# Attention rounds of a fused kernel: second score pieces behind the transposes, a fourth output buffer, GpSimd work tied to later VectorE steps

## The chip, the cores and the metric

The kernel runs on one core of a Trainium2 chip. The metric is device time in microseconds (us). The kernel before took 706.64 us (median of three runs, 706.31 to 711.38).

## The reference: what is computed

An attention with a learned position bias feeds a feed-forward layer with a rational activation:

```python
scores = scale * q @ k.T                     # batch 4, heads 8, sequence 576, head width 64
bias = relu(psi(i, j) * w1 + b1) @ w2        # one value per pair of positions and head
attn = exp(scores + bias - rowmax)
attn = attn / (attn.sum(-1) + 1e-9)
x = (attn @ v)                               # as 2304 tokens x 512
h = x @ w_in                                 # 512 -> 2048
P = a0 + a1 h + a2 h^2 + a3 h^3
Q = 1 + |b0| |h| + |b1| h^2
out = (P / (Q + 1e-6)) @ w_out               # 2048 -> 512
```

## The kernel before, in words

The program has three parts: bias tables (up to about 50 us), attention, and the feed-forward layer. The change touches the attention part alone. All order is written out by hand (`manual_schedule`): each engine runs its instructions in the order in which the program text issues them, and waits inside that order.

**Units and steps.** A unit is a pair of heads of one batch element; there are 16 (`NU`). Two units share nine steps (`UPG = 9`): the even unit has five blocks of query rows (`c` from 0 to 4), the odd one four, because the fifth step carries the last 64 rows of both units (step 4 of nine, "the shared step"). So there are 72 steps (`NS`), and `rnd(r)` handles two, `i = 2r` and `i + 1`; rounds 1 to 35 are the attention's main loop.

**One round.** TensorE does, in this order: scores of step i and the long pieces of the scores of step i+1 (`e_qk`, L346; 576 columns are cut into 448 and 128 because they lie across two PSUM banks); then 32 transposes of the probabilities of steps i-2 and i-1 (`e_tp`, L433; the two halves of the rows, r = 0 and 1, are woven so that they can run side by side), with small ones for the tail columns and, where a unit has ended, for its row sums; the short second pieces (128 columns) of the scores of step i+1 stand among them; then the products with v for steps i-3 and i-2 (`e_pv`, L492). VectorE adds the bias and takes the row maximum (`e_ttr`, L365, one per head and step: four in a round), copies tail columns and row sums out of PSUM (`put_tails`, L460 and L469), turns sums into reciprocals (L389, L390) and copies products out of PSUM into the output buffer `xs` (L501). ScalarE does the exponentials (L379) and copies the transposes out of PSUM (L448).

**Output buffers.** Each unit has a tile `xs` of 128x576 in a pool of three buffers. It is filled a block at a time over its steps; when its row sums have come back from DRAM as `rb`, GpSimd multiplies it by them (`e_norm`, L414, in two halves of 288 columns, each in a round of its own), and SyncE (SP) sends it to DRAM as `xd` (L416). The first copy into the `xs` of a later unit waits until the transfer of the unit three before has left the buffer. A unit's product for an even step is put at the start of the next round (`puts`), that of an odd step near the end of its round.

**Weight passes.** Between these, from round 4 to round 33, weights of the feed-forward layer are split into a high and a low part, one pair of jobs (a, b) in three rounds (`job_plan`, phases 0, 1, 2). The passes of a job are: `mag` (VectorE, L156), `rebias` (ScalarE, L165), `sign` (VectorE, L168), `mid` (GpSimd, L177), `join` (VectorE, L181) and `low` (GpSimd, L188). VectorE's `sign` and `join` each read two tiles in SBUF. `behind(x, op)` makes a GpSimd instruction x wait for the VectorE instruction op, so that it doesn't run beside what stands ahead of it.

**Order of VectorE before, in a round:** put of the even step's product; early weight passes; the two `e_ttr` of step i; the two of step i+1; tails and sums; reciprocals; put of the odd step's product; later weight passes.

Of the kernel before, what the change touches and what calls it, by code (L numbers as in the profile page):

```python
# [9 lines left out]
F32 = mybir.dt.float32  # L10
# [7 lines left out]
P = 128  # L18
# [19 lines left out]
def tile_attn_moe(  # L38
# [91 lines left out]
    def w_conv(f, part):  # L130
# [36 lines left out]
        def sign():  # L167
            V.scalar_tensor_tensor(  # L168
                out=st["wh"], in0=rows(st["u"]), scalar=0x80000000, in1=st["wh"],
                op0=ALU.bitwise_and, op1=ALU.bitwise_or,  # L170
            )
# [61 lines left out]
    with tc.manual_schedule():  # L233
# [3 lines left out]
        with ExitStack() as actx:  # L237
# [121 lines left out]
            def e_ttr(i, j):  # L359
# [4 lines left out]
                o0 = strip(i, j)  # L364
                on(V.tensor_tensor_reduce(  # L365
                    out=t, in0=WF[:, o0:o0 + S], in1=bias[p][:, 5 * j + c, :],
                    scale=-0.125, scalar=3.0e38,
                    op0=ALU.add, op1=ALU.min, accum_out=m,
                ), o0 // 512, o0 // 512 + 1)
                s2[i, j] = (t, m)  # L370

            def e_exp(i, j):
# [34 lines left out]
            def e_norm(u):  # L407
# [10 lines left out]

                if eng is V:
                    return [lambda: part(0, S)]  # L420
                return [lambda: part(0, SH), lambda: part(SH, S)]

# [58 lines left out]
            def e_pv(i, b):  # L481
# [13 lines left out]
                for x in zs:  # L495
                    if x not in xs:
                        xs[x] = npool.tile([P, S], F32, tag="xs", name=f"xs{x}", bufs=3)

# [39 lines left out]
            def done_to(k):  # L538
                g, c = divmod(k, UPG)
                u = 2 * g - 2  # L540
                if g > 0:
                    if c == 1 and u != NX or k == NS:
                        norms.extend(e_norm(u))
                    if c == 6 and g * 2 < NU:
                        norms.extend(e_norm(u + 1))
                    if c == 2 and u + 1 < NU - 1:
                        load_rb(u + 1)
# [20 lines left out]
            def job_plan(r):  # L568
                q, ph = divmod(r - 4, 3)
                c = 2 * q  # L570
                if r < 4 or c >= len(jobs):
                    return [], [], [], [], []
                a, b = jobs[c], jobs[c + 1]
# [12 lines left out]
                if ph == 0:  # L586
                    return a[1], a[2], [a[4]], [a[3][0], hi(a)], []
                if ph == 1:
                    return [a[3][1]] + b[1], b[2], [a[3][2], b[4]], [b[3][0], hi(b)], [out(c)]
                return [b[3][1]], [], [b[3][2]], [], [out(c + 1)]  # L590

            ZZ = (4, 1)

            def rnd(r):
                i = 2 * r
                early, act, pool, later_, outs = job_plan(r)
# [4 lines left out]
                for x in early:  # L601
                    op = x() or op
                for x in act:
                    x()
# [34 lines left out]
                if put:  # L639
                    put()  # L640
                for x in later_ + list(hi[1:]) + outs:
                    x()
# [431 lines left out]
```

## Time and profile before

| what | us |
|---|---|
| median of three runs | 706.64 |
| profiled execution | 708.67 |
| its span, first to last instruction | 706.9 |
| rounds 2 to 35 of the attention | 246.99 |
| from the end of round 35 to the end | 404.00 |

The profiled execution was 2.03 us (0.3%) slower than the median, and 1.8 us of it lie outside the span. Round numbers are those of `rnd(r)`; a round is counted from the first of its scores on TensorE to the first of the next round's. In the views, PE is TensorE, DVE VectorE, ACT ScalarE, POOL GpSimd; a release in square brackets tells how long the engine had been idle and what ended it.

### The profile page before, as it was taken

To read this page: it belongs to the slowest core of one execution; us is meant where nothing else is said; L and a number is where in the kernel's file an instruction comes from. 1 tells how busy PE (TensorE), PEld (TensorE's weight loads), DVE (VectorE), ACT (ScalarE), POOL (GpSimd) and SP (SyncE) were. 2 spreads that over 40 slices of the span, in tenths; PEclk is the share of its full clock that TensorE was granted. 3 is DMA by queue.
4 is the path that set the end of the run, shared out by engine and by line. 5 is a ranking of instruction groups with operands and counts; after the bars stand their busy time and mean duration, and the time that the engine had idled before them with its cause. 6 is when DMAs were issued, how large, how long until landed. Compare 5 with 4: busy or idle time off the path is not lost.

```text
span 706.9 us, 16149 instructions
## 1 busy us (share of the span) xinstructions
PE 672.3 (95%) x6274; PEld 551.5 (78%) x6274; DVE 557.0 (79%) x1030; ACT 474.0 (67%) x758; POOL 155.4 (22%) x122
## 2 busy tenths in 40 slices
PE   9999969898988878999999999999999999999997
PEld 6657758667776657798888888899998888888896
DVE  7986867677756757749999898988877968779766
ACT  7979867777767758866676756656666564555551
POOL 0000223132312323202222212131221221221221
PEclk9999998999989989999999999999999999999999
DMA  6987766667667747643365361766850121303031
GB/s 232 307 315 241 247 187 227 196 223 209 203 184 253 230 165 221 201 132 121 116 183 190 118 207 48 254 209 203 301 181 29 59 105 60 104 1 119 1 105 45
DMA packets 74844, 118.97 MB, mean 168 GB/s; under 512 B 11904, under 2 KB 33808, under 8 KB 74768
## 3 DMA queue, kind: packets, MB, share of 16 engines
q1 hardware_dynamic: 74624, 117.79, 50.7%
q8 instruction: 49, 0.80, 0.5%
q14 instruction: 27, 0.22, 0.1%
q10 hardware_dynamic: 144, 0.16, 0.1%
HBM read 79.17 MB, written 35.61 MB: 162 GB/s over the span
## 4 chain that ended last, share of the span: by engine, by line
PE 61%; DMA 2%; DVE 1%; issue 1%; SPq 1%; POOL 0%; DVEq 0%
PE ps L316 28%; PE ps L903 28%; PE ps L492 2%; DMA xd<-xs 2%; PE ps L346 1%; PE ps L433 1%; DVE s L365 1%; DVE xs L501 0%; DVE wh L168 0%; POOL wm L177 0%; SPq L140 0%; SPq L128 0%; DVE wk L156 0%; DVE wm L181 0%; DVE pre L924 0%
## 5 line engine op out<-in xcount | busy, mean ns | idle before, releaser
L873 POOL TENSOR_TENSOR gl<-m,r 128x1024 fp32r<-128x1024 f32 (+1 forms) x39 | 85.6, 2195 | 300.0 <-DVE m L866 267.8
L365 DVE CUSTOM_DVE_ANT_0 s<-ps,bias 128x576 f32<-128x576 f32 x144 | 106.1, 756 | 23.6 <-PE ps L433 10.9
L346 PE MATMUL ps<-k,q 64*128 64x448 f32 (+3 forms) x640 | 108.3, 431 | 6.9 <-DVE m L365 6.7
L824 ACT ACTIVATE w<-ps,babs 128x1024 f32<-128x1024 f32 (+1 forms) x40 | 41.3, 1031 | 107.6 <-PE ps L316 104.0
L379 ACT ACTIVATE p<-s,m 128x576 f32<-128x576 f32 x144 | 110.1, 778 | 2.6 <-DVE m L365 2.6
L448 ACT COPY pt<-ps 128x512 f32<-128x512 f32 (+1 forms) x109 | 73.0, 730 | 42.0 <-PE ps L433 41.6
L433 PEld LDWEIGHTS ps<-ident,p 64*128 64x128 f32 x1296 | 62.4, 145 | 41.6 <-issue 33.4
L433 PE MATMUL ps<-ident,p 64*128 64x64 f32 x1296 | 68.7, 233 | 21.6 <-DVE xs L501 21.6
L492 PE MATMUL ps<-pt,v 128*64 128x128 f32 (+1 forms) x1280 | 85.4, 281 | 0.3 <-ACT pt L448 0.3
L903 PE MATMUL ps<-wol,gh 128*128 128x512 f32 x216 | 84.2, 390 | 0.0
L903 PE MATMUL ps<-woh,gh 128*128 128x512 f32 x216 | 84.2, 390 | 0.0
L346 PEld LDWEIGHTS ps<-k,q 64*128 64x128 f32 (+1 forms) x640 | 54.7, 178 | 31.9 <-issue 18.2
L836 DVE SCALAR_TENSOR_TENSOR u<-w,babs,ps 128x1024 f32<-128x1024 f32 (+1 forms) x40 | 46.9, 1172 | 38.1 <-ACT t L825 38.0
L492 PEld LDWEIGHTS ps<-pt,v 128*64 128x64 f32 x1280 | 71.8, 146 | 3.2 <-ACT pt L448 0.4
L316 PE MATMUL ps<-xb,wih 128*128 128x512 f32 (+1 forms) x240 | 68.8, 367 | 0.0
L501 DVE COPY xs<-ps 128x128 f32<-128x128 f32 (+1 forms) x80 | 21.0, 266 | 60.5 <-DMA xd<-xs 36.1
L831 ACT ACTIVATE u<-u 128x1024 f32<-128x1024 f32 (+1 forms) x40 | 39.1, 977 | 40.2 <-DVE u L836 40.1
L852 DVE SCALAR_TENSOR_TENSOR gh<-t,cst,r 128x1024 fp32r<-128x1024 f32 (+1 forms) x40 | 46.9, 1174 | 9.3 <-ACT r L833 6.9
L903 PE MATMUL ps<-woh,gl 128*128 128x512 f32 x216 | 53.8, 389 | 0.0
L859 DVE SCALAR_TENSOR_TENSOR m<-u,qc,gh 128x1024 f32<-128x1024 f32 (+1 forms) x40 | 47.1, 1178 | 4.0
L316 PEld LDWEIGHTS ps<-xb,wih 128*128 128x128 f32 x240 | 44.5, 188 | 6.1
L866 DVE SCALAR_TENSOR_TENSOR m<-t,cst,m 128x1024 f32<-128x1024 f32 (+1 forms) x40 | 47.1, 1178 | 1.4
(81 smaller groups left out, 1351.7 us busy)
## 6 DMA issues: line engine op xcount, KB each, us to landing
tab<-e SPq DMA_DIRECT2D x36, 295.5 KB, 3.2
wx<-in_w_in_dram SPq DMA_DIRECT2D x16, 512.0 KB, 5.0
wx<-in_w_out_dram SPq DMA_DIRECT2D x16, 512.0 KB, 4.5
v<-in_vp_dram SPq DMA_DIRECT2D x16, 320.0 KB, 3.7
ws<-wh SPq DMA_DIRECT2D x20, 256.0 KB, 2.0
ws<-wl SPq DMA_DIRECT2D x20, 256.0 KB, 3.1
q<-in_qt_dram SPq DMA_DIRECT2D x16, 288.0 KB, 3.6
k<-in_kt_dram SPq DMA_DIRECT2D x16, 288.0 KB, 4.6
```

What stands on the lines that cost most here:

```text
L316: on(T.matmul(hps[s][:, j, :w_], w[:, k, sl], x[:, k, :w_], start=(k == 0 and z == 0), stop=(k == KD - 1 and z == 2),), b + j)
L346: on(T.matmul(WF[o, o0 + a:o0 + z], q[r, x], k[r, a:z], start=True, stop=True), (o0 + a) // 512)
L365: on(V.tensor_tensor_reduce(out=t, in0=WF[:, o0:o0 + S], in1=bias[p][:, 5 * j + c, :], scale=-0.125, scalar=3.0e38, op0=ALU.add, op1=ALU.m ...
L379: A.activation(out=prob[i][:, z * S:z * S + S], in_=t, func=AF.Exp, bias=m, scale=-1.0, accum_out=sums[u % 4][:, k:k + 1],)
L433: on(T.transpose(W[:, b, o:o + 64], src[x, :], ident[x, x]), b)
L448: on(A.copy(out=t.rearrange("p x (r s) -> p r x s", r=2)[:, a:z], in_=W[:, to[a]:to[a] + z - a].rearrange("p r (x s) -> p r x s", s=64),), ...
L492: on(T.matmul(ps[y, o], vt[n][:, kc, y], w_, start=(kc == 0), stop=(kc == 4)), b, mem=(f"pt{i % 3}", f"tl{i // 2 % 2}"))
L836: on(V.scalar_tensor_tensor(out=et(s, "u", 2), in0=rt[s, "w"], scalar=babs[:, 0:1], in1=hp(s), op0=ALU.add, op1=ALU.mult,), *hb(s), mem="wu")
L859: V.scalar_tensor_tensor(out=m, in0=rt[s, "u"], scalar=qc, in1=rt[s, "gh"].bitcast(F32), op0=ALU.add, op1=ALU.mult,)
L866: V.scalar_tensor_tensor(out=m, in0=rt[s, "t"], scalar=abs_[:, 0:1], in1=m, op0=ALU.add, op1=ALU.subtract)
L873: eng.tensor_tensor(out=lo, in0=rt[s, "m"], in1=rt[s, "r0"], op=ALU.mult)
L903: on(T.matmul(po[n, c], l[:, j, c * P:(c + 1) * P], r[fp][:, j, :], start=(first and x is a), stop=(last and x is z),), OB[c])
```

## The change

- The short second pieces of the scores of step i+1 go behind all transposes of the round, for both halves of the rows.
- `xs` has four buffers.
- GpSimd normalises a unit in one instruction of 576 columns; an even unit's is queued one step earlier (c = 0); GpSimd takes none in a round of phase 2 while there are weight jobs.
- `join` goes behind the two `e_ttr` of step i ("second"). `sign` of job b goes from the end of phase 1 to the start of phase 2, and `mid` of b from phase 1 to phase 2.
- `mid` of a, and both `low`, are tied behind the last VectorE instruction of that second place (`pool2`).
- The tails and sums are copied between the two `e_ttr` of step i+1.

```diff
-                if eng is V:
-                    return [lambda: part(0, S)]
-                return [lambda: part(0, SH), lambda: part(SH, S)]
+                return [lambda: part(0, S)]
...
-                        xs[x] = npool.tile([P, S], F32, tag="xs", name=f"xs{x}", bufs=3)
+                        xs[x] = npool.tile([P, S], F32, tag="xs", name=f"xs{x}", bufs=4)
...
-                    if c == 1 and u != NX or k == NS:
+                    if c == 0 and u != NX or k == NS:
                         norms.extend(e_norm(u))
...
                 if ph == 0:
-                    return a[1], a[2], [a[4]], [a[3][0], hi(a)], []
-                if ph == 1:
-                    return [a[3][1]] + b[1], b[2], [a[3][2], b[4]], [b[3][0], hi(b)], [out(c)]
-                return [b[3][1]], [], [b[3][2]], [], [out(c + 1)]
+                    plan.update(first=a[1], act=a[2], pool2=[a[4]], third=[a[3][0], hi(a)])
+                elif ph == 1:
+                    plan.update(first=b[1], act=b[2], second=[a[3][1]], pool2=[a[3][2]], outs=[out(c)])
+                else:
+                    plan.update(
+                        first=[b[3][0]], pool=[b[4]], second=[b[3][1]], pool2=[b[3][2]],
+                        outs=[hi(b), out(c + 1)],
+                    )
+                return plan
...
-                ops = pool + ([norms.pop(0)] if norms else [])
-                for x in ops:
+                if not plan["pool"] and norms:
+                    plan["pool"].append(norms.pop(0))
+                for x in plan["pool"]:
                     x = x()
-                    if op is not None and x is not None:
+                    if op is not None:
                         behind(x, op)
                 for j in range(2):
-                    e_ttr(i, j)
+                    op = e_ttr(i, j)
+                for x in plan["second"]:
+                    op = x()
+                for x in plan["pool2"]:
+                    behind(x(), op)
+                small = [ends[r] + ends_[r] + adds[r] for r in range(2)]
                 weave(
-                    main[0][:4] + sb[0][1:] + ends[0] + ends_[0] + adds[0] + main[0][4:] + main_[0],
-                    main[1] + main_[1] + sb[1][1:] + ends[1] + ends_[1] + adds[1],
+                    main[0] + small[0] + main_[0] + sb[0][1:],
+                    main[1] + main_[1] + small[1] + sb[1][1:],
                 )
...
-                for j in range(2):
-                    e_ttr(i + 1, j)
+                e_ttr(i + 1, 0)
                 put_tails(i - 2, 2, ZZ, us)
+                e_ttr(i + 1, 1)
```

What moves, in the order of the instructions on the engines:

TensorE, round 20, from the long score pieces (128x448) to the first products with v (L492); p_3060 and p_3063 (in the change p_3054 and p_3057) are the probabilities of steps 38 and 39. Before, its last rows:

```order
L433 MATMUL ps<-ident,p_3060 128x64
L433 MATMUL ps<-ident,p_3063 128x64
L433 MATMUL ps<-ident,p_3060 128x64
L433 MATMUL ps<-ident,p_3063 128x64 x6
L346 MATMUL ps<-k_2608,q_2607 128x128
L433 MATMUL ps<-ident,p_3063 128x64 x4
L433 MATMUL ps<-ident,p_3060 128x64
L433 MATMUL ps<-ident,p_3063 128x64 x2
L492 MATMUL ps<-pt_2965,v_2487 64x128 x8
```

and with the change, all of it:

```order
L346 MATMUL ps<-k_2604,q_2603 128x448 x2
L432 MATMUL ps<-ident,p_3054 128x64 x17
L432 MATMUL ps<-ident,p_3057 128x64 x16
L432 MATMUL ps<-ident,p_3054 128x64
L432 MATMUL ps<-ident,p_3057 128x64 x2
L346 MATMUL ps<-k_2604,q_2603 128x128 x2
L491 MATMUL ps<-pt_2959,v_2481 64x128 x8
```

The two pieces of 128x128 stood after 8 and after 29 transposes, and now stand together at the end.

VectorE, from the `sign` of job a in round 22 (phase 0) into round 23 (phase 1: steps 46 and 47). Before:

```order
L168 SCALAR_TENSOR_TENSOR wh6_0_3309<-wx6_0_2953,wh6_0_3309 128x512
L501 COPY xs9_3288<-ps_91 128x128
L181 SCALAR_TENSOR_TENSOR wm6_0_3319<-wm6_0_3319,wh6_0_3309 128x512
L156 TENSOR_SCALAR wk6_1_3425<-wx6_1_3178 128x512
L365 ISA s2_46_0_3442,m46_0_3443<-ps_91,bias2_1910 128x576
L365 ISA m46_0_3443 128x1
L365 ISA s2_46_1_3445,m46_1_3446<-ps_91,bias2_1910 128x576
L365 ISA m46_1_3446 128x1
L365 ISA s2_47_0_3489,m47_0_3490<-ps_91,bias2_1910 128x576
```

and with the change:

```order
L168 SCALAR_TENSOR_TENSOR wh6_0_3302<-wx6_0_2947,wh6_0_3302 128x512
L500 COPY xs9_3280<-ps_91 128x128
L156 TENSOR_SCALAR wk6_1_3417<-wx6_1_3169 128x512
L365 ISA s2_46_0_3431,m46_0_3432<-ps_91,bias2_1908 128x576
L365 ISA m46_0_3432 128x1
L365 ISA s2_46_1_3434,m46_1_3435<-ps_91,bias2_1908 128x576
L365 ISA m46_1_3435 128x1
L181 SCALAR_TENSOR_TENSOR wm6_0_3318<-wm6_0_3318,wh6_0_3302 128x512
L365 ISA s2_47_0_3481,m47_0_3482<-ps_91,bias2_1908 128x576
L365 ISA m47_0_3482 128x1
L459 COPY tl44_3484<-ps_91 128x2x64 x2
L365 ISA s2_47_1_3487,m47_1_3488<-ps_91,bias2_1908 128x576
```

`join` (L181) went from ahead of the step's first `e_ttr` to behind its second, and the tail copies stand between the two of step 47.

GpSimd, rounds 22 to 24: weight passes of job pair 6 and the normalisation of unit 7. Before:

```order
L177 COPY wm6_0_3319<-wx6_0_2953 128x1024
L188 TENSOR_TENSOR wl6_0_3437<-wm6_0_3319,wh6_0_3309 128x512
L177 COPY wm6_1_3439<-wx6_1_3178 128x1024
L414 TENSOR_TENSOR xs7_2822<-xs7_2822,rb7_3180 128x288
L188 TENSOR_TENSOR wl6_1_3550<-wm6_1_3439,wh6_1_3427 128x512
L414 TENSOR_TENSOR xs7_2822<-xs7_2822,rb7_3180 128x288
```

and with the change:

```order
L177 COPY wm6_0_3318<-wx6_0_2947 128x1024
L415 TENSOR_TENSOR xs7_2815<-xs7_2815,rb7_3171 128x576
L188 TENSOR_TENSOR wl6_0_3438<-wm6_0_3318,wh6_0_3302 128x512
L177 COPY wm6_1_3539<-wx6_1_3169 128x1024
L188 TENSOR_TENSOR wl6_1_3548<-wm6_1_3539,wh6_1_3419 128x512
```

The two halves, in rounds 23 and 24, became one instruction in round 23, ahead of `low` of a.

## Rows read from the trace of the kernel before

**Rows 1.** The page: busy time and share of the span of TensorE.
```profile
PE 672.3 (95%) x6274; PEld 551.5 (78%) x6274; DVE 557.0 (79%) x1030; ACT 474.0 (67%) x758; POOL 155.4 (22%) x122
```

**Rows 2.** Waits of the whole execution: engine, line, awaited, total us, times, longest.
```profile
DVE xs L501 <- DMA xd<-xs: 36.1, 10, 6.3
...
PE ps L433 <- DVE xs L501: 21.6, 11, 4.9
...
PE ps L346 <- DVE m L365: 6.7, 12, 1.0
```

**Rows 3.** Stretches: us, busy PE, PEld, DVE, ACT, POOL, granted clock, DMA, GB/s.
```profile
55.91:302.90 246.99, 219.18 (x3384) 174.07 (x3382) 172.34 (x541) 187.76 (x402) 66.60 (x66) 0.94 0.67 213
302.90:706.90 404.00, 399.89 (x1922) 341.61 (x1922) 336.13 (x356) 239.05 (x276) 87.14 (x41) 1.00 0.38 126
86.38:92.26 5.88, 5.88 (x94) 4.76 (x92) 4.91 (x16) 5.56 (x13) 1.80 (x2) 1.00 0.66 213
79.44:86.38 6.94, 6.94 (x104) 5.03 (x103) 5.03 (x16) 5.19 (x12) 1.28 (x1) 1.00 0.71 209
229.08:235.04 5.96, 5.96 (x116) 4.84 (x114) 5.10 (x17) 5.71 (x13) 3.09 (x3) 1.00 0.95 300
249.59:263.15 13.56, 8.84 (x102) 7.05 (x100) 5.50 (x16) 7.63 (x17) 3.08 (x3) 0.75 0.34 129
```

**Rows 4.** Timeline of TensorE in round 7: start, us, engine, line, operation.
```profile
86.38 2.00 PE L346 MATMUL ps<-k,q 64*128 64x448 f32 x12
88.21 0.41 PE L433 MATMUL ps<-ident,p 64*128 64x64 f32 x8
...
88.83 0.83 PE L433 MATMUL ps<-ident,p 64*128 64x64 f32 x18
...
89.93 1.09 PE L492 MATMUL ps<-pt,v 128*64 128x128 f32 x16
```

**Rows 5.** Timeline of VectorE in round 7.
```profile
86.78 0.42 DVE L156 TENSOR_SCALAR wk<-wx 128x512 uint32<-128x512 uint32 x1
87.77 0.76 DVE L365 CUSTOM_DVE_ANT_0 s<-ps,bias 128x576 f32<-128x576 f32 x1 [0.57 <-PE ps L346]
...
88.45 0.75 DVE L365 CUSTOM_DVE_ANT_0 s<-ps,bias 128x576 f32<-128x576 f32 x1
...
89.24 0.76 DVE L365 CUSTOM_DVE_ANT_0 s<-ps,bias 128x576 f32<-128x576 f32 x1
...
90.83 0.48 DVE L460 COPY tl<-ps 128x128 f32<-128x128 f32 x2
91.23 0.16 DVE L389 TENSOR_SCALAR sum<-sum 128x10 f32<-128x10 f32 x1
...
91.56 0.24 DVE L501 COPY xs<-ps 128x128 f32<-128x128 f32 x1
91.72 0.68 DVE L168 SCALAR_TENSOR_TENSOR wh<-wx,wh 128x512 uint32<-128x512 uint32 x1
```

**Rows 6.** Timeline of VectorE and TensorE in round 29.
```profile
255.03 0.29 DVE L501 COPY xs<-ps 128x128 f32<-128x128 f32 x1 [5.33 <-DMA xd<-xs]
...
255.46 0.52 PE L433 MATMUL ps<-ident,p 64*128 64x64 f32 x8 [3.72 <-DVE xs L501]
...
259.20 1.97 PE L492 MATMUL ps<-pt,v 128*64 128x128 f32 x16
```

**Rows 7.** Tensor xd: time from the issue of its transfers to landing.
```profile
DMA to landing us min/median/max: 2.3/3.0/6.9
```

**Rows 8.** GpSimd's normalisation (line 414), and VectorE beside the longest of them.
```profile
L414 POOL TENSOR_TENSOR xs<-xs,rb x28: 795/804/1192, 88.3 to 308.2; 128x288 f32<-128x288 f32 x28
...
296.23 0.55 DVE L301 TENSOR_TENSOR xl<-xs,xh 128x384 fp32r<-128x384 f32 x1
296.24 1.95 POOL L414 TENSOR_TENSOR xs<-xs,rb 128x288 f32<-128x288 f32 x2 [9.33 <-DMA rb<-rs]
```

**Rows 9.** Groups of VectorE in the attention: busy us, mean ns; idle before.
```profile
L469 DVE COPY rt<-ps 10x64 f32<-10x64 f32 (+1 forms) x30 | 5.0, 202 | 0.0
```

More of the change, by code (lines that the diff above doesn't have):

```diff
@@ L167, in sign @@
         def sign():
-            V.scalar_tensor_tensor(
+            return V.scalar_tensor_tensor(
                 out=st["wh"], in0=rows(st["u"]), scalar=0x80000000, in1=st["wh"],
@@ L364, in e_ttr @@
                 o0 = strip(i, j)
-                on(V.tensor_tensor_reduce(
+                op = on(V.tensor_tensor_reduce(
                     out=t, in0=WF[:, o0:o0 + S], in1=bias[p][:, 5 * j + c, :],
@@ L370, in e_ttr @@
                 s2[i, j] = (t, m)
+                return op
             def e_exp(i, j):
@@ L570, in job_plan @@
                 c = 2 * q
+                plan = {k: [] for k in ("first", "act", "pool", "second", "pool2", "third", "outs")}
                 if r < 4 or c >= len(jobs):
-                    return [], [], [], [], []
+                    return plan
                 a, b = jobs[c], jobs[c + 1]
@@ L586, in job_plan @@
                 if ph == 0:
-                    return a[1], a[2], [a[4]], [a[3][0], hi(a)], []
-                if ph == 1:
-                    return [a[3][1]] + b[1], b[2], [a[3][2], b[4]], [b[3][0], hi(b)], [out(c)]
-                return [b[3][1]], [], [b[3][2]], [], [out(c + 1)]
+                    plan.update(first=a[1], act=a[2], pool2=[a[4]], third=[a[3][0], hi(a)])
[6 more added lines that the diff above has]
+                    )
+                return plan
             ZZ = (4, 1)
@@ L595, in rnd @@
                 i = 2 * r
-                early, act, pool, later_, outs = job_plan(r)
+                plan = job_plan(r)
                 loads(i)
@@ L600, in rnd @@
                     op = puts.pop(0)()
-                for x in early:
-                    op = x() or op
-                for x in act:
+                for x in plan["first"]:
+                    op = x()
+                for x in plan["act"]:
                     x()
@@ L609, in rnd @@
                 weave(sa[0] + sb[0][:1], sa[1] + sb[1][:1])
-                ops = pool + ([norms.pop(0)] if norms else [])
-                for x in ops:
+                if not plan["pool"] and norms:
+                    plan["pool"].append(norms.pop(0))
+                for x in plan["pool"]:
                     x = x()
-                    if op is not None and x is not None:
+                    if op is not None:
                         behind(x, op)
                 for j in range(2):
-                    e_ttr(i, j)
+                    op = e_ttr(i, j)
+                for x in plan["second"]:
+                    op = x()
+                for x in plan["pool2"]:
+                    behind(x(), op)
+                small = [ends[r] + ends_[r] + adds[r] for r in range(2)]
                 weave(
-                    main[0][:4] + sb[0][1:] + ends[0] + ends_[0] + adds[0] + main[0][4:] + main_[0],
-                    main[1] + main_[1] + sb[1][1:] + ends[1] + ends_[1] + adds[1],
+                    main[0] + small[0] + main_[0] + sb[0][1:],
+                    main[1] + main_[1] + small[1] + sb[1][1:],
                 )
@@ L640, in rnd @@
                     put()
-                for x in later_ + list(hi[1:]) + outs:
+                for x in plan["third"] + list(hi[1:]) + plan["outs"]:
                     x()
```

## The prediction

> **What bounds the kernel now.** I read the page first: TensorE is busy for 95% of the span [rows 1], which looks as if nothing could be gained by moving other engines' work. That share is an average over stages, so I cut the span next. From the end of round 35 on, TensorE is busy for 399.89 of 404.00 us at a granted clock of 1.00; rounds 2 to 35 take 246.99 us, with TensorE busy for 219.18 and a clock of 0.94 [rows 3]. The change touches only these 34 rounds. The view of waits then says what is awaited there: VectorE's copies into xs waited ten times for a transfer xd<-xs, 36.1 us in all, and TensorE's transposes eleven times for such a copy, 21.6 us [rows 2]. The timeline shows why the one follows from the other. In round 29 the put of the last round's product finds its output buffer still being sent, VectorE stands for 5.33 us, and the transposes, which go into the bank that this put empties, stand for 3.72 us [rows 6]. After it TensorE is slow as well: 16 products took 1.97 us, against 1.09 in a round without the wait, and the mean clock over round 29 was 0.75, so part of it ran at the lower of the two levels (1.2 instead of 2.4 GHz) [rows 3, 4, 6]. That round took 13.56 us.
>
> A round without the wait takes 5.88 (round 7) or 5.96 us (round 26), TensorE busy all through [rows 3]. Of round 7, 1.83 us are scores, 1.72 the transposes with the short score pieces (88.21 to 89.93), 2.33 the products [rows 3, 4]. With 5.9 for each, 34 rounds would take 200.6 us; 46.4 us are above that. Four rounds of 6.94, in which step i+1 is the shared one, hold 4.2 us of it [rows 3]; I put the remaining 42 down to the ten waits, what the clock gives away after them, and a few tenths of other waits, such as TensorE's 6.7 us for row maxima [rows 2].
>
> **The change part by part.** *Four buffers.* Before, the copy that waits wants the buffer of the unit three before; the second half of that unit's normalisation stands in the same round or the one ahead, and after it a transfer that lands 2.3 to 6.9 us after its issue [rows 7]. With four buffers, the first copy into unit u+4 waits for unit u. Counted in rounds of the program, unit 0 is normalised in round 7 and its buffer wanted at the start of round 11; unit 1 in round 10, wanted at the start of round 13; unit 3 in 14 and at the end of 17; so at least two and a half rounds, nearly 15 us, lie between, against 1.6 us of GpSimd, the longest landing of 6.9, and SP's queue. I take all ten waits as gone: 42 us at most. What is late next is VectorE itself, below.
>
> *One normalisation.* Twice 804 ns becomes about 1.6 us, the same work [rows 8]. It hides beside the row maxima, which leave GpSimd 3 of 5.9 us a round [rows 3]. On SP the transfer moves up a round at most; the DMAs behind it in SP's queue (stores of weights, loads) then stand until GpSimd is done, and are wanted rounds later: nothing.
>
> *Short score pieces last.* All instructions stay. What counts is how much of TensorE's work stands behind the second row maximum of step i, since the transposes of step i-1 go into banks that it reads. In round 7 that maximum ends at 89.20 and the products begin at 89.93 [rows 4, 5]. Behind it stood 12 transposes and a score piece, and now 16 and two pieces that can run side by side, one for each half of the rows. A transpose goes by in 34 ns (18 between 88.83 and 89.44 [rows 4]), so this costs between 0 and 0.2 us a round; I take 0.1, or 3.4 us for 34. In the four rounds with the shared step the two pieces no longer stand apart; I take 0.7 us above a normal round for each instead of 1.05, so 2.8 us.
>
> *VectorE's order.* Now the first maximum of step i+1 needs the last thing that TensorE does before its products, at about 3.75 us into the round instead of 2.86 (89.24 minus 86.38 [rows 5]). In phases 1 and 2 `join`, 0.68 us like `sign`, fills the gap; in phase 0 nothing does. There the chain runs on: maximum to 4.5, tails 0.48, second maximum to 5.7, sums or reciprocals 0.33 to 0.40 in nearly every round, a put 0.24, `sign` 0.68 [rows 5, 9]. That ends at 7.0; the next put and `mag` bring it to 7.7, and the next round's first maximum starts at 1.8 into its round instead of 1.39 (87.77 [rows 5]). So each of the ten rounds after a phase 0 loses 0.38 us: 3.8. In phases 1 and 2 the chain ends near 6.3 to 6.4, and put and `sign` or `mag` are over before 1.39: nothing.
>
> *GpSimd's ties.* `mid` of b (about 1 us) now stands in the same round as the `join` that needs it, behind `sign`. It has the two maxima, 1.5 us [rows 5], as cover. The long normalisation begins behind `mag` and, if `mag` is late, is still running when `join` starts in phase 1, six times. The one case in the trace of GpSimd beside a VectorE instruction that reads two tiles in SBUF is at 296.23: that half took 1192 ns instead of 804, VectorE kept its 0.55 us [rows 8]. So they do hinder each other, and here `join` would be the one that comes second. Between 0 and 0.4 us each; I take 1.0 us in all. The Trainium skill speaks against the change here: by "SBUF — State Buffer", section "Who interferes with whom", a VectorE instruction with two inputs in SBUF and a GpSimd instruction that reads SBUF exclude each other, and the later one stands until the other is through. The trace agrees in direction, 0.39 us longer, less than VectorE's whole 0.55. By that rule the whole overlap would be paid and the time is the forecast; with no such interference it would be 1.0 us less.
>
> **The sum.** 200.6 + 3.4 + 2.8 + 3.8 + 1.0 = 211.6 us for rounds that took 246.99: 35.4 less. Against the profiled execution's own 708.67 that gives 673.3; it was 2.03 above the median of the runs, and on the median's scale the forecast is 706.64 - 35.4 = **671.2 us**.
>
> **The rivals.**
>
> *VectorE becomes the bound, slower than before.* Holding the first maximum of step i+1 back until the last score piece puts the engines in a ring: put 0.24, `sign` 0.68, two maxima 1.51, the transposes with the pieces 1.72 less what runs ahead of the second maximum (about 0.75 left), maximum 0.76, tails 0.48, sums 0.40, maximum 0.76, reciprocals 0.33 (91.23 to 91.56), put 0.24, `sign` 0.68 [rows 4, 5, 9]: 6.8, and some 0.1 at each of seven handovers: 7.5 us. If every round ran so, 34 would take 255.0, 8.0 more than now: 715 us. It decides from 7.26 us a round (246.99 / 34). Against it: VectorE is busy for 4.91 and 5.10 us in such rounds [rows 3], and no round holds all these parts. Chance 0.05.
>
> *Another wait takes the buffer's place.* The rounds come closer together, so the DMA share of 0.67 grows to about 0.78, and it is already 0.95 in round 26 [rows 3]; a late weight load, bias load or `rb` would stand where the transfer stood. If half of the 42 us stays: 671.2 + 21 = 692 us. Against it: rounds 7 and 26 ran at full pace at shares of 0.66 and 0.95. Chance 0.11.
>
> *The change doesn't do what it says.* If the transfer were late by SP's queue rather than by buffers, the four buffers would fill up as three did, and only the new order's costs and small gains would remain: 703 to 712 us. Against it stands the count of rounds above. Chance 0.05.
>
> *More than I think.* If the new order costs nothing and transposes in these rounds are shorter, at 5.75 us a round (ScalarE is busy for 5.56 of 5.88 [rows 3]) and 2.1 for the shared steps, 34 rounds take 197.6: 657 us. Chance 0.09.
>
> **How the numbers follow.** The forecast's own case, all ten waits gone and rounds of 5.85 to 6.6 us, has 0.70; its bounds are 200.6 + 2.1 (706.64 - 44.3 = 662) and 34 x 6.6 + 2.8 (706.64 - 19.8 = 687). The range reaches a little below, into the last rival: 659 to 687. Faster by over 1% (about what a measurement of this kernel tells from no change) are the forecast, the second and the last rival: 0.90; within 1% are the third rival: 0.05; slower the first: 0.05.
>
> **What would show it.** In the profile of the changed kernel: the wait of VectorE's xs copies for xd<-xs gone, and with it TensorE's wait for them; the clock of rounds 2 to 35 near 1.00; 13 or 14 normalisations of about 1.6 us; VectorE's idle time ahead of line 365 longer, ended by TensorE, most in phase 0; rounds of phase 1 some 0.4 us longer than those of phases 0 and 2. Wrong it would be if xs still waits, if `join` waits for GpSimd by more than a few us in all, if TensorE waits for row maxima by far more than 6.7 us, or if rounds without any wait take other than about 6 us.

## The result and the profile after

The changed kernel takes 672.66 us (median of four runs, 671.91 to 674.15) against 708.33 (706.31 to 711.38) for the kernel before on the same chip: a ratio of 0.9496, interval 0.945 to 0.9541. The forecast was 671.2 us, and faster. The profiled execution took 674.15 us, the longest of the four; its span is 672.4. Line numbers have moved by one: L433, L492, L501, L460, L448, L414 and L379 of before are L432, L491, L500, L459, L447, L415 and L380 now.

First the page of the changed kernel, the line of busy times that answers to [rows 1]:

```profile
PE 657.0 (98%) x6274; PEld 537.2 (80%) x6274; DVE 554.0 (82%) x1030; ACT 474.8 (71%) x758; POOL 153.2 (23%) x108
```

The number of instructions of TensorE is the same, its busy time is 15.3 us less: the same work at a higher clock, as the stretches show. The first row is rounds 2 to 35, the second the rest to the end; then round 7, a round with the shared step, and round 29 (columns as in [rows 3]):

```profile
56.21:267.45 211.24, 202.81 (x3374) 159.04 (x3374) 168.64 (x540) 187.97 (x401) 64.64 (x53) 1.00 0.78 250
267.45:672.40 404.95, 400.70 (x1938) 342.10 (x1934) 336.94 (x360) 239.83 (x276) 86.96 (x40) 1.00 0.38 126
86.97:93.10 6.13, 5.86 (x94) 4.65 (x92) 4.58 (x18) 5.82 (x15) 2.45 (x2) 1.00 0.77 239
80.73:86.97 6.24, 6.24 (x104) 4.60 (x103) 5.03 (x17) 4.96 (x13) 2.31 (x2) 1.00 0.68 218
222.27:230.33 8.06, 6.16 (x102) 4.63 (x100) 5.46 (x16) 5.13 (x12) 2.67 (x2) 1.00 0.99 365
```

All of the gain lies in the 34 rounds: 246.99 us before, 211.24 now, 35.75 less. The part behind them is 0.95 longer, and round 2 begins 0.30 later. The granted clock over the 34 rounds went from 0.94 to 1.00 [rows 3].

The view of waits of the changed kernel (engine, line, what was awaited: us in total, times, longest):

```profile
DVE s L365 <- PE ps L346: 33.2, 42, 2.5
...
PE ps L432 <- DVE m L365: 6.4, 26, 0.3
...
ACT wh L165 <- DMA ws<-wh: 2.9, 1, 2.9
...
PE ps L432 <- DVE xs L500: 0.7, 2, 0.6
```

The line DVE xs <- DMA xd<-xs, 36.1 us and ten times in [rows 2], is gone, and of TensorE's 21.6 us behind it 0.7 are left. Two things are new. The first is a small wait in most rounds: TensorE's transposes stand about 0.25 us for a row maximum, 26 times. The timelines of round 7 show where, TensorE first and VectorE's first three maxima after it:

```profile
86.97 2.00 PE L346 MATMUL ps<-k,q 64*128 64x448 f32 x12
88.80 0.78 PE L432 MATMUL ps<-ident,p 64*128 64x64 f32 x20
89.85 0.71 PE L432 MATMUL ps<-ident,p 64*128 64x64 f32 x16 [0.27 <-DVE m L365]
90.40 0.44 PE L346 MATMUL ps<-k,q 64*128 64x128 f32 x4
90.77 1.09 PE L491 MATMUL ps<-pt,v 128*64 128x128 f32 x16
```

```profile
88.35 0.76 DVE L365 CUSTOM_DVE_ANT_0 s<-ps,bias 128x576 f32<-128x576 f32 x1 [0.33 <-PE ps L346]
...
89.04 0.75 DVE L365 CUSTOM_DVE_ANT_0 s<-ps,bias 128x576 f32<-128x576 f32 x1
...
90.98 0.76 DVE L365 CUSTOM_DVE_ANT_0 s<-ps,bias 128x576 f32<-128x576 f32 x1 [1.18 <-PE ps L346]
```

The second maximum ends at 89.79, 2.82 us into the round, exactly as before (89.20 minus 86.38 [rows 3, 5]). Before, transposes and short pieces ran on while it ran, and TensorE was busy for all 5.88 us of the round. Now 20 transposes are done at 89.58, the next one may not begin before the maximum is over, and everything else stands behind it in the queue: TensorE stands 0.27 us. Its work is the same (5.86 us), and the products begin 3.80 us into the round instead of 3.55. The short pieces had been the filler for this wait. VectorE, in turn, now stands 1.18 us for the pieces.

The second new thing is one long round, 29. ScalarE and then TensorE there:

```profile
226.75 0.72 ACT L165 ACTIVATE wh<-wk,wmin 128x512 uint32<-128x512 uint32 x1 [2.93 <-DMA ws<-wh]
227.38 1.97 ACT L447 COPY pt<-ps 128x512 f32<-128x512 f32 x3
```

```profile
226.00 0.44 PE L346 MATMUL ps<-k,q 64*128 64x128 f32 x4
228.00 1.09 PE L491 MATMUL ps<-pt,v 128*64 128x128 f32 x16 [1.56 <-ACT pt L447]
```

`rebias` of a weight job (L165) stands 2.93 us until the store of an earlier `wh` has left its tile. Behind it on ScalarE are the copies of the transposes, and the products wait for these. The tiles `wh` are a pool of two, one for jobs a and one for jobs b, and round 29 is a phase 1, with the `rebias` of a job b. So the tile that it needs is that of job b of the pair before, whose store SyncE had issued at 219.70 only:

```profile
219.70 0.43 SPq L128 DMA_DIRECT2D ws<-wh  x1
```

The change itself put this store late: `sign` of job b and its store went from the end of phase 1 to phase 2. It went out 2.57 us before round 29 began (222.27); with four buffers alone, the first experiment below, the same store went out 6.55 us before (at 212.46, round 29 at 219.01). And it was slow: `rebias` began 7.05 us after its issue, where transfers from `wh` landed after 2.0 to 7.4 us, 3.1 on the median; the DMA share of round 29 is 0.99.

### The profile page after: what moved, and what is told of

The parts are those of the page before. It is cut to its first block, busy times and chain, and to the rows that moved or that the text cites. A ratio compares the mean times of both kernels' runs of the same rounds, so it can differ in the third digit from the quotient of the medians.

```text
span 672.4 us, 16098 instructions
## 1 busy us (share of the span) xinstructions
PE 657.0 (98%) x6274; PEld 537.2 (80%) x6274; DVE 554.0 (82%) x1030; ACT 474.8 (71%) x758; POOL 153.2 (23%) x108
## 4 chain that ended last, share of the span: by engine, by line
PE 66%; DVE 4%; DMA 3%; issue 1%; ACT 1%; SPq 0%; DVEq 0%
PE ps L316 29%; PE ps L914 29%; PE ps L491 3%; DVE s L365 3%; PE ps L346 2%; PE ps L432 2%; DMA ws<-wh 2%; DMA wx<-in_w_out_dram 1%; DVE xs L500 0%; ACT p L380 0%; DVE tl L459 0%; ACT pt L447 0%; DVE sum L390 0%; DVE m L365 0%; DVE wk L156 0%
## 5 line engine op out<-in xcount | busy, mean ns | idle before, releaser
L380 ACT ACTIVATE p<-s,m 128x576 f32<-128x576 f32 x144 | 110.1, 773 | 2.6 <-DVE m L365 2.6
L447 ACT COPY pt<-ps 128x512 f32<-128x512 f32 (+1 forms) x109 | 74.4, 727 | 22.7 <-PE ps L432 22.2
L346 PE MATMUL ps<-k,q 64*128 64x448 f32 (+3 forms) x640 | 89.8, 425 | 0.2 <-DVE m L365 0.2
L491 PE MATMUL ps<-pt,v 128*64 128x128 f32 (+1 forms) x1280 | 78.2, 265 | 1.8 <-ACT pt L447 1.8
L432 PEld LDWEIGHTS ps<-ident,p 64*128 64x128 f32 x1296 | 49.8, 138 | 28.0 <-DVE m L365 10.6
L491 PEld LDWEIGHTS ps<-pt,v 128*64 128x64 f32 x1280 | 65.1, 137 | 6.7 <-ACT pt L447 2.2
L432 PE MATMUL ps<-ident,p 64*128 64x64 f32 x1296 | 55.0, 225 | 7.4 <-DVE m L365 6.4
L346 PEld LDWEIGHTS ps<-k,q 64*128 64x128 f32 (+1 forms) x640 | 43.5, 176 | 21.7 <-issue 16.6
L856 DVE SCALAR_TENSOR_TENSOR t<-t,cst,ps 128x1024 f32<-128x1024 f32 (+1 forms) x40 | 47.0, 1175 | 1.4
```

Source lines behind the costliest of these rows:

```text
L346: on(T.matmul(WF[o, o0 + a:o0 + z], q[r, x], k[r, a:z], start=True, stop=True), (o0 + a) // 512)
L380: A.activation(out=prob[i][:, z * S:z * S + S], in_=t, func=AF.Exp, bias=m, scale=-1.0, accum_out=sums[u % 4][:, k:k + 1],)
L432: on(T.transpose(W[:, b, o:o + 64], src[x, :], ident[x, x]), b)
L447: on(A.copy(out=t.rearrange("p x (r s) -> p r x s", r=2)[:, a:z], in_=W[:, to[a]:to[a] + z - a].rearrange("p r (x s) -> p r x s", s=64),), ...
L491: on(T.matmul(ps[y, o], vt[n][:, kc, y], w_, start=(kc == 0), stop=(kc == 4)), b, mem=(f"pt{i % 3}", f"tl{i // 2 % 2}"))
L856: on(V.scalar_tensor_tensor(out=rt[s, "t"], in0=rt[s, "t"], scalar=abs_[:, 1:2], in1=hp(s), op0=ALU.add, op1=ALU.mult,), *hb(s), mem="t")
```

## The experiments

Two theories stood at first. **A**: the gain is the fourth output buffer, and the rest of the change costs more than it brings. Its **rival**: the new order is needed for the gain. Later ones ask what the rest costs (D: whether VectorE's new order belongs to the new order of TensorE; E and F: what makes `rebias` wait). Each ratio is to the kernel before on the chip of that run.

**The fourth buffer alone** (the kernel before with one number changed).

```diff
-                        xs[x] = npool.tile([P, S], F32, tag="xs", name=f"xs{x}", bufs=3)
+                        xs[x] = npool.tile([P, S], F32, tag="xs", name=f"xs{x}", bufs=4)
```

> The kernel before with one edit: four xs buffers. Theory A (the gain of the change is the buffer wait alone, and the late score pieces cost about 0.2 us a round): the wait of xs for xd is gone, rounds go back to 5.9 and the four shared ones stay at 6.94, so 34 rounds take about 206 us instead of 247: 666 us, some 6 us faster than the whole change (672.7). Theory B (the order of VectorE and the single normalisation are needed as well): part of the ten waits stays, 680 to 695 us.

Measured: 667.39 us, ratio 0.9423 (0.939 to 0.9457). Its stretches, rounds 2 to 35, a shared round and round 7:

```profile
56.30:261.72 205.42, 204.88 (x3384) 163.50 (x3382) 172.21 (x541) 185.46 (x401) 66.13 (x66) 1.00 0.81 255
79.83:86.77 6.94, 6.94 (x105) 5.03 (x103) 5.03 (x16) 5.19 (x12) 1.28 (x1) 1.00 0.73 205
86.77:92.64 5.87, 5.87 (x94) 4.75 (x92) 4.91 (x16) 5.55 (x13) 1.80 (x2) 1.00 0.70 217
```

There is no wait for xd, and the rounds take what the undisturbed rounds of before took. 246.99 - 205.42 = 41.57 us are the price of the ten waits with all that hung on them; the prediction had put down 42. A stands: this one number gives more than the whole change. Its six runs (667.19 to 668.4) all lie below the fastest of the change (671.91), though the intervals of the two ratios overlap a little.

**The change with three buffers**, that is, everything except the buffer.

```diff
-                        xs[x] = npool.tile([P, S], F32, tag="xs", name=f"xs{x}", bufs=4)
+                        xs[x] = npool.tile([P, S], F32, tag="xs", name=f"xs{x}", bufs=3)
```

> The whole change, but with three xs buffers. Theory A1 (a wait was 6.3 us at most, a round is 6.1, and the single normalisation sends most units a round earlier): most of the ten waits are gone without the fourth buffer as well, at most a few us remain: 672 to 678 us. Theory A2 (only the fourth buffer takes the waits away): ten waits of some 3 to 6 us come back, 695 to 705 us.

Measured: 693.88 us, ratio 0.9801 (0.9761 to 0.984). Its waits, and round 20:

```profile
DVE xs L500 <- DMA xd<-xs: 17.3, 6, 5.2
```

```profile
172.57:186.55 13.98, 9.33 (x102) 7.19 (x100) 5.55 (x16) 7.28 (x17) 2.67 (x2) 0.76 0.69 224
```

Neither reading written down came out: six of ten waits are back, with about half of their time. So without the fourth buffer the rest of the change takes four waits of ten away. The normalisation in one piece, up to a round earlier, is the likely reason, but no run has it alone, and the rounds here are longer too. With four buffers there is no such wait under either order, so that earlier start has nothing left to bring. A stall costs more than its length: in round 20 (VectorE's copy waited 5.2 us) TensorE is busy 9.33 us, at a clock of 0.76, with work that takes it 5.8 to 6.2 elsewhere.

**The change with the short pieces where they were.**

```diff
-                    main[0] + small[0] + main_[0] + sb[0][1:],
-                    main[1] + main_[1] + small[1] + sb[1][1:],
+                    main[0][:4] + sb[0][1:] + ends[0] + ends_[0] + adds[0] + main[0][4:] + main_[0],
+                    main[1] + main_[1] + sb[1][1:] + ends[1] + ends_[1] + adds[1],
```

> The whole change, but with the short score pieces among the transposes as before. Theory A (rounds of 6.13 instead of 5.9 come from the pieces at the end): rounds fall to about 5.9, the four shared ones rise to about 6.9, together 5 us less: 667 us. Theory C (the 6.13 come from the order of VectorE, with the tails between two row maxima): no change, 672 us.

Measured: 671.87 us (667.23 to 674.22), ratio 0.9482 (0.9437 to 0.9527). In the profiled execution (668.21 us) the normal rounds take 5.82 to 5.97 again (but for rounds 2 and 4, 6.02 and 6.54) and the shared ones 6.93 to 6.95, so the 0.25 us a round are the pieces. But the gain did not arrive in the median: the runs lie 7 us apart, and round 29 took 7.10 us with the wait for the store in it:

```profile
ACT wh L165 <- DMA ws<-wh: 1.6, 1, 1.6
```

**Four buffers and pieces last, VectorE's order as before.**

```diff
+                small = [ends[r] + ends_[r] + adds[r] for r in range(2)]
                 weave(
-                    main[0][:4] + sb[0][1:] + ends[0] + ends_[0] + adds[0] + main[0][4:] + main_[0],
-                    main[1] + main_[1] + sb[1][1:] + ends[1] + ends_[1] + adds[1],
+                    main[0] + small[0] + main_[0] + sb[0][1:],
+                    main[1] + main_[1] + small[1] + sb[1][1:],
                 )
```

> The kernel before with two edits: four xs buffers and the short score pieces behind the transposes; VectorE, GpSimd and the normalisation in halves as before. Theory A (the pieces' place alone makes a round 6.13): as the whole change, 672 to 675 us. Theory D (with the pieces last, VectorE's old order, join ahead of the row maxima and sign at the end, becomes the bound in phases 0 and 1, as the prediction priced it): rounds of 6.3 to 6.7 us, 678 to 690 us.

Measured: 681.25 us, ratio 0.9617 (0.9583 to 0.9651); 13.9 more than the fourth buffer alone. Rounds 2 to 35 and two of them, round 8 (phase 1) and round 7 (phase 0):

```profile
56.35:274.89 218.54, 209.11 (x3382) 159.69 (x3382) 166.24 (x539) 189.23 (x400) 66.05 (x66) 1.00 0.75 241
94.67:101.28 6.61, 6.29 (x116) 4.85 (x115) 5.42 (x19) 5.78 (x13) 3.07 (x3) 1.00 0.77 222
88.38:94.67 6.29, 6.02 (x95) 4.64 (x93) 4.32 (x17) 5.65 (x13) 1.79 (x2) 1.00 0.75 238
```

VectorE in round 8:

```profile
95.44 0.69 DVE L181 SCALAR_TENSOR_TENSOR wm<-wm,wh 128x512 uint32<-128x512 uint32 x1
...
96.39 0.75 DVE L365 CUSTOM_DVE_ANT_0 s<-ps,bias 128x576 f32<-128x576 f32 x1
...
99.01 0.76 DVE L365 CUSTOM_DVE_ANT_0 s<-ps,bias 128x576 f32<-128x576 f32 x1 [1.19 <-PE ps L346]
...
100.38 0.48 DVE L460 COPY tl<-ps 128x128 f32<-128x128 f32 x2
```

Theory D holds. `join` at the start puts the first maximum at 1.72 us into the round (1.38 in the change's rounds 7 and 8), and the tails, behind both late maxima, come at 5.71 and hold the last products. While VectorE stands 1.19 us for the pieces, `join` could have run there. That is what the change's VectorE order does. Of the 13.1 us that its TensorE order costs here (218.54 against 205.42 for the rounds), the rest of the change wins back 7.3 (211.24), round 29 and its late store included; that VectorE's part of it does this, and not GpSimd's, is read from these rows and not shown by a run of its own. With the old TensorE order it has hardly anything to win, as the experiment before showed.

**Four buffers, pieces last only in the four shared rounds.**

```diff
+                if steps[i + 1][1] == 4:
+                    weave(
+                        main[0] + small[0] + main_[0] + sb[0][1:],
+                        main[1] + main_[1] + small[1] + sb[1][1:],
+                    )
+                else:
...
```

> Four buffers and the order of before, with the short score pieces behind the transposes only in the four rounds whose step i+1 is the shared one. Theory A (in these rounds the pieces of 64 columns cannot run beside transposes, so standing together at the end they cost less): the four rounds fall from 6.94 to about 6.3, the others stay at 5.9: 665 us, 2.4 below four buffers alone. Rival: VectorE's old order makes these rounds or the next ones longer again, as it did with the pieces last everywhere: 667 to 668 us.

Measured: 664.97 us, ratio 0.939 (0.9362 to 0.9419). A shared round:

```profile
79.37:85.76 6.39, 6.39 (x104) 4.58 (x103) 4.92 (x16) 5.43 (x14) 1.28 (x1) 1.00 0.69 205
```

A again: all other rounds stay at 5.83 to 6.23, and the shared ones drop from 6.94 to 6.39. That is the part of the reordering that pays. The difference is small, and the ratios' intervals overlap; it rests on the rounds (203.30 us against 205.42) and on run times that don't overlap (664.93 to 666.16, against 667.19 to 668.4).

**The store of job b right behind its `sign`**, at the start of phase 2 instead of its end. Three versions: with TensorE's old order, with the change's, and with pieces last in shared rounds only.

```diff
+                    def sign_out():
+                        op = b[3][0]()
+                        hi(b)()
+                        return op
+
                     plan.update(
-                        first=[b[3][0]], pool=[b[4]], second=[b[3][1]], pool2=[b[3][2]],
-                        outs=[hi(b), out(c + 1)],
+                        first=[sign_out], pool=[b[4]], second=[b[3][1]], pool2=[b[3][2]],
+                        outs=[out(c + 1)],
                     )
```

> The whole change with the short score pieces in their old place, and the store of the high part of job b issued right behind its sign instead of at the end of phase 2. Theory E (the runs of 667 to 674 us without it come from ScalarE's rebias, which waits for the late store to leave its buffer): all runs within 1 us, 666 to 667.5 us, no wait of line 165 for ws<-wh. Rival (other transfers, such as the weight loads wx, make the spread): the spread stays, median 669 to 672 us.

> The whole change with the store of the high part of job b issued right behind its sign. Theory E: round 29 falls from 8.06 to about 6.1 us, all others stay: 670.7 us. Rival (that wait is only moved to another transfer): 672 to 673 us.

> The whole change with the early store, and the short score pieces behind the transposes only in the four rounds with the shared step. Theories A and E together: 30 rounds of 5.9 and four of about 6.25 us: 664 us, below four buffers alone (667.4). Rival (the order of VectorE or GpSimd adds a wait of its own that the longer rounds hid): 667 us or more.

Measured: 672.25 us, ratio 0.9486 (0.9453 to 0.9519); 678.81, 0.9586 (0.9542 to 0.963); 671.8, 0.9468 (0.9429 to 0.9507). Theory E fell as it was framed: the waits of L165 are longer, not gone. Those of the second version:

```profile
ACT wh L165 <- DMA ws<-wh: 4.0, 1, 4.0
...
ACT wh L165 <- DMA woh<-wh: 2.6, 2, 2.5
```

SyncE's queue says why the edit could not help. The store of one `wh` (job b of rounds 7 to 9), first in the kernel with four buffers alone, then in the change, then in the second version:

```profile
103.55 0.49 SPq L196 DMA_DIRECT2D woh<-wh  x1
```

```profile
108.02 0.49 SPq L196 DMA_DIRECT2D woh<-wh  x1
```

```profile
97.97 5.99 SPq L260 DMA_DIRECT2D bias<-tab  x6
...
110.81 0.49 SPq L196 DMA_DIRECT2D woh<-wh  x1
```

In the last two the order of the queue around it is the same: a weight load, four loads of `rb`, v, q and k, and then the store. SyncE issues nothing between the two places in this round, nor in round 27, whose store round 29 waits for, so moving the store between them changes nothing. And SyncE runs late: in the second version six bias loads took 5.99 us from the first issue to the end of the last, against 5.31 in the change and 4.93 with four buffers alone, and the store went out 11.1 us after the start of round 9 (99.73), in the change 8.7 us after (99.31), with four buffers alone, where it stands at the end of round 8, 4.9 us after (98.61).

**`sign` of b and its store back at the end of phase 1**, the rest as in the change.

```diff
                 elif ph == 1:
-                    plan.update(first=b[1], act=b[2], second=[a[3][1]], pool2=[a[3][2]], outs=[out(c)])
-                else:
                     plan.update(
-                        first=[b[3][0]], pool=[b[4]], second=[b[3][1]], pool2=[b[3][2]],
-                        outs=[hi(b), out(c + 1)],
+                        first=b[1], act=b[2], second=[a[3][1]], pool2=[a[3][2]],
+                        third=[b[3][0], hi(b)], outs=[out(c)],
                     )
+                else:
+                    plan.update(pool=[b[4]], second=[b[3][1]], pool2=[b[3][2]], outs=[out(c + 1)])
```

> The whole change, but sign of job b and the store of its high part stand at the end of phase 1 again, as before; the pieces stay last. Theory F (SP runs up to a round late, so a store that is queued in phase 2 lands too late for ScalarE's rebias two rounds on, whose buffer it reads): no wait of line 165 for a store, round 29 at 6.1 us, runs within 1.5 us of each other, 670 to 671 us. Rival (the waits come from a busy DMA whatever the store's place): 672 to 679 us with a spread of several us.

Measured: 671.52 us (671.44 to 672.5), ratio 0.9498 (0.947 to 0.9526). No wait of L165 is left, round 29 takes 6.09 us, and the six runs lie within 1.1 us. Theory F stands: the wait and the spread come from `sign` and its store in phase 2, and cost 3.0 us beside the change on the same chip (674.52, below). Rounds 2 to 34 but for 29 take what they take in the change, within 0.01 us.

**The same with pieces last in shared rounds only** (the two edits above together).

> As the run before, and the pieces last only in the four rounds with the shared step. Theories A and F: 30 rounds of 5.9 and four of 6.3 to 6.4 us, as with four buffers and the hybrid alone (665.0): 664 to 665 us; VectorE's new order then gains nothing, since TensorE sets these rounds. Rival (VectorE's new order is worth something by itself): 662 us or less.

Measured: **663.68 us** (663.24 to 665.59), ratio 0.9388 (0.9362 to 0.9415); the lowest median of all, and 10.8 us under the change on the same chip (674.52, below). From four buffers with pieces last in shared rounds (664.97) its runs don't tell it apart; the rounds do, 201.89 us against 203.30. Rounds 2 to 35, a shared round and round 29:

```profile
55.58:257.47 201.89, 201.89 (x3384) 161.56 (x3382) 168.14 (x541) 185.05 (x401) 64.80 (x53) 1.00 0.81 258
79.24:85.48 6.24, 6.24 (x104) 4.61 (x102) 5.00 (x17) 5.28 (x14) 2.32 (x2) 1.00 0.66 186
215.81:221.64 5.83, 5.83 (x102) 4.56 (x101) 5.13 (x16) 5.59 (x13) 2.70 (x2) 1.00 0.98 303
```

TensorE is busy for every microsecond of the 34 rounds. With the change's order of VectorE and GpSimd a shared round takes 6.24 us, not 6.39, and rounds 23 and 32 take 5.89 and 5.88, not 6.23 and 6.14: so that order is worth 1.4 us by itself, less than the rival named, and not the nothing that was expected.

**Four buffers alone, but `sign` of b and its store in phase 2.**

```diff
-                    return [a[3][1]] + b[1], b[2], [a[3][2], b[4]], [b[3][0], hi(b)], [out(c)]
-                return [b[3][1]], [], [b[3][2]], [], [out(c + 1)]
+                    return [a[3][1]] + b[1], b[2], [a[3][2], b[4]], [], [out(c)]
+                return [b[3][0], b[3][1]], [], [b[3][2]], [], [hi(b), out(c + 1)]
```

> Four buffers alone (667.4 us, runs within 1.3 us), with one more edit: sign of job b and the store of its high part go from the end of phase 1 into phase 2, as in the change. Theory F: waits of rebias for a store appear near rounds 11 and 29, with a spread of some us: 668 to 674 us. Rival (the place of the store is innocent): 667 to 668 us.

Measured: 671.78 us (670.58 to 676.08), ratio 0.9508 (0.9477 to 0.954), against 667.39 (667.19 to 668.4) without this edit. Its waits:

```profile
PE ps L346 <- DVE m L365: 3.0, 8, 0.7
...
ACT wh L165 <- DMA ws<-wh: 0.9, 1, 0.9
...
ACT wh L165 <- DMA woh<-wh: 0.5, 1, 0.5
```

The late store brings waits of L165 and a spread to the kernel before too, as F said. But in the profiled execution, the fastest of the six (670.58), they are the small part: rounds 11 and 29 are 0.5 us longer than with four buffers alone, and the ten rounds of phase 2 together 3.3. `sign` and `join` now both stand ahead of the maxima of a phase 2, and the scores wait for these. What the slower executions waited for, no trace shows.

**The change once more**, unaltered, on the chip of the last three.

> The whole change unaltered, beside the others on one chip. If the 678.8 us of the version with the early store came from that edit: 672 to 674 us here. If it came from the chip or its transfers on that day, since the order of SP is nearly the same: 675 us or more, with waits of rebias for stores of several us.

Measured: 674.52 us (672.89 to 677.24), ratio 0.9544 (0.9513 to 0.9574), round 29 again with 2.9 us of wait for ws<-wh. The interval of the early store's second version (0.9542 to 0.963) overlaps with this one, so whether that version is slower than the change at all stays open, and with it why SyncE's bias loads took longer there.

## Why the prediction was right, and which of its terms were not

The mechanism was the one forecast, and the sum came out: 211.6 us for the 34 rounds, 211.24 measured. Terms in it were off in both directions, and they cancelled; that the sums agree to 0.4 us is luck:

| term | predicted, us | measured, us | how measured |
|---|---|---|---|
| 34 rounds at 5.9 | 200.6 | 200.6 | kept as the base |
| short pieces last | 3.4 | 7.1 | 30 rounds, 0.24 each: the 28 without another cause take 6.14 on the mean |
| shared rounds | 2.8 | 1.3 | four of 6.23 to 6.24 |
| VectorE's chain after phase 0 | 3.8 | 0 | phases 0, 1, 2 alike, 6.08 to 6.21 |
| GpSimd beside `join` | 1.0 | under 0.1 | below |
| `rebias` waits for a late store | none | 1.9 | round 29, 8.06 against 6.14 |
| round 32 | none | 0.3 | 6.42 against 6.14; it stood out before as well, 6.13 against 5.9 |
| sum | 211.6 | 211.2 | |

- *All ten waits gone, 42 us.* Right: 41.57 by the buffer alone. The count of rounds between the normalisation and the next use held.
- *Short score pieces last, 0.1 us a round.* The idea was right (what counts is the work behind the second maximum), the size wrong, and the measured 0.24 lies outside the bounds of 0 and 0.2. In round 7, 0.98 us (89.79 to 90.77) now stand behind the end of the maximum, against 0.73 before (89.20 to 89.93 [rows 4, 5]): the handover, 16 transposes in 0.55 us and the pieces in 0.37. The estimate let the two pieces, side by side, cost almost nothing. Before, transposes of the other half of the rows ran beside each piece (a piece at 88.58, three transposes from 88.59 on); now nothing does, and what the pieces had filled is idle.
- *VectorE's chain, 3.8 us.* This step failed. Its start was nearly right: the maximum of step i+1 begins 4.01 us into round 7 (90.98), forecast about 3.75. What went wrong is the end. After that round, a phase 0, the last thing ahead of the next first maximum, and that maximum:

```profile
94.02 0.42 DVE L156 TENSOR_SCALAR wk<-wx 128x512 uint32<-128x512 uint32 x1
...
94.48 0.76 DVE L365 CUSTOM_DVE_ANT_0 s<-ps,bias 128x576 f32<-128x576 f32 x1
```

  The chain is over 7.47 us after the round's start (94.44), forecast 7.7; and the forecast took off 5.9 us for the round, which is 6.13 long. So the maximum begins 1.38 us into its round, as it does in the others, and not 1.8: about half of the difference is the shorter chain, and half the longer round. A longer round of one engine is slack for the other: the costs of the pieces and of the chain could not simply be added. That VectorE was near was right all the same. With its old order the rounds take 218.54 us; and in round 32, where the chain from round 31 (a phase 0) holds one pass more, the first maximum begins 1.69 us into the round (242.66) and the round takes 6.42 us:

```profile
243.35 0.54 DVE L301 TENSOR_TENSOR xl<-xr,xh 128x384 fp32r<-128x384 f32 x1
...
244.35 0.74 DVE L365 CUSTOM_DVE_ANT_0 s<-ps,bias 128x576 f32<-128x576 f32 x1
```
- *Shared rounds, 0.7 above a normal one.* They are only 0.10 above it. In round 6, the first of two such groups with four buffers alone, and the one group in the change:

```profile
82.30 0.44 PE L346 MATMUL ps<-k,q 64*64 64x128 f32 x4
```

```profile
84.26 0.45 PE L346 MATMUL ps<-k,q 64*64 64x128 f32 x8
```

  All eight pieces together take as long as a group of four had taken, and the transposes are no longer broken up by them. The 0.70 us that a shared round saves is the only thing that this reordering brings; 0.55 of it come with TensorE's order alone (6.39 above).
- *GpSimd's ties, 1.0 us.* One instruction of 576 columns is shorter than forecast and than two halves of 804 ns; in the main loop it is mostly over, or within 0.1 us of its end, when `join` begins:

```profile
L415 POOL TENSOR_TENSOR xs<-xs,rb x14: 1407/1414/1418, 88.1 to 273.2; 128x576 f32<-128x576 f32 x14
```

In round 32 `join` does begin 0.20 us before it ends (244.50 + 1.41), and takes 0.76 us instead of 0.69:

```profile
244.50 1.41 POOL L415 TENSOR_TENSOR xs<-xs,rb 128x576 f32<-128x576 f32 x1 [3.99 <-DVE wk L156]
```

```profile
245.71 0.76 DVE L181 SCALAR_TENSOR_TENSOR wm<-wm,wh 128x512 uint32<-128x512 uint32 x1
```

So the second to come was delayed by 0.07 us. The Trainium skill, "SBUF — State Buffer", section "Who interferes with whom", would have it stand for the whole overlap, 0.20; the row agrees in direction and in who pays, with a third of the size. A longer overlap agrees better. In the change with three buffers a VectorE pass over two tiles (L301) begins 0.24 us after such a multiplication and takes 1.59 us instead of 0.55, so it pays 1.04 of the 1.17 us that remained:

```profile
282.56 1.41 POOL L415 TENSOR_TENSOR xs<-xs,rb 128x576 f32<-128x576 f32 x1 [7.46 <-DMA rb<-rs]
```

```profile
282.80 1.59 DVE L301 TENSOR_TENSOR xl<-xs,xh 128x384 fp32r<-128x384 f32 x1
```

In both cases, and in the prediction's own (0.39 of 0.54 [rows 8]), what was paid is the overlap less 0.13 to 0.15 us; `join`s that met the last 0.11 us or less of a multiplication were not delayed. The term is small because `join` hardly ever met one, not because meeting is cheap.

- *The DMAs moved in SP's queue: nothing.* Failed, and here a rival came true in small. The prediction asked when the moved transfers are wanted, but did not ask it of the store of `wh` that the change delays: the next job's `rebias` needs its tile. "Another wait takes the buffer's place" had named late weight transfers; its price was 1.9 us in this profile, not 21. The delay of this store had no term in the sum at all.
- *VectorE becomes the bound* did not occur in the change, and no round came near 7.26 us but for round 29. *The change doesn't do what it says*: it does. *More than I think* named 657 us; the lowest median of the versions here is 663.68. The lower end of the forecast's own case was worked out with rounds of 5.9 us, not with the 5.85 that it names; with these it would have been 661, not 662.

Against the fourth buffer alone the whole change loses 5.82 us in the rounds: 29 rounds with pieces last +6.50, round 29 +2.15, four shared rounds -2.83.

## What to carry to other kernels

When a copy waits for a transfer to leave its buffer, try one more buffer by itself before any reordering: here that gave more than the whole change. An instruction that fills an engine's wait is not free to move, even if all the work stays; look at what the engine would do in that place without it. When a write is moved later, ask who needs its source tile next, and read the time of the transfer from the queue that issues it, not from its place in the program.

## What the runs showed of the hardware

- Without the stalls TensorE's granted clock was 1.00 over all the rounds. With three buffers it was 0.76 over a round in which VectorE's copy waited 5.2 us, and that round took 13.98 us instead of the 6.08 of the change with four: TensorE stood for 4.65 us, and its own work took 9.33 us instead of 6.02, in part at the lower of the two levels.
- One GpSimd multiplication of 128x576 took 1414 ns, two of 128x288 804 each: the one is 0.19 us shorter than the two.
- Score pieces on 64 rows and 64 columns (64*64 in the rows) took as much time in a group of eight as in a group of four, 0.45 and 0.44 us.
- GpSimd multiplications and VectorE passes that each read two tiles in SBUF hold each other up: in the cases above, whichever came second took longer by the overlap less 0.13 to 0.15 us.
- SyncE's queue is itself a resource: in the rounds of the change one issue took 0.3 to 2.2 us, half of them under 0.5, and a store went out up to 11 us after the start of the round in whose text it stands.
